# Seven block products for the second product of a pair of chunks, with the output weights held still

## The chip, the core and the metric

The kernel runs on one core of a Trainium2 chip. The metric is the device time of a run in microseconds (us). The core's engines work side by side and meet at semaphores: TensorE (PE, matrix products; PEld is its loading of the stationary operand), VectorE (DVE), ScalarE (ACT), GpSimd (POOL) and SyncE (SP), which issues nearly all DMA transfers here, in order.

## The reference

```
q_s = softmax of q over the head dimension      # 8 batches, 8 heads, 576 positions, 64
k_s = softmax of k over the positions
kv  = einsum('bhsd,bhse->bhde', k_s, v)
x   = einsum('bhsd,bhde->bhse', q_s, kv), heads side by side: 4608 x 512
h   = max(x @ w1, x @ w2, x @ w3)               # 768 wide
out = h @ w_out                                 # 4608 x 512, float32
```

All is float32. A product of float32 accuracy is made of three matmuls in a faster 32-bit format: each operand is split into a high part (a copy that rounds) and a low part (the difference), and low x high, high x low and high x high are summed.

## The kernel before

The 4608 rows are worked in nine chunks of 512: chunk c holds the first 512 positions of batch c, and the ninth the 64 left-over positions of all batches. Attention for a batch is done on VectorE, ScalarE, GpSimd and small matmuls, and it produces x, turned (features on partitions), for its chunk.

Chunks 0 to 2 (class Chunk) go the plain way: gate (L1049 to L1055) multiplies x with the three weights, hidden takes the maximum, and second_product (L1085 on) makes four tiles of 128 rows by 512 outputs, each of 6 x 3 matmuls. In these the piece of h is stationary and the split output weights wo (oh, ol) stream.

Chunks 3 to 8 go in three pairs (class Duo). There the product of the gate weights with both chunks is a 2 x 2 block product made of seven block products P1 to P7 in place of eight (Winograd's form of Strassen's scheme): convert makes the seven combinations of x (xb), mix_weights the combinations of weights, which go to DRAM (keep_s) beside copies of the plain split weights (keep_a); weights loads one 256 KB tile for each product into a ring of eight slots (ws), and products (L1276) issues six matmuls for each. There are nine units u of a weight and a pair of column blocks: unit u gives its four maxima once outcome has added and compared the seven results in PSUM (L1302 to L1324, on ScalarE and VectorE). The maxima stay in mm, 2 chunks x 6 column blocks x 512 rows. The second product of a pair was plain: hidden (L1362, L1364) splits mm into a ring of three tiles hs (the third one lies in the tile mix), and second multiplies each of eight tiles of 128 rows with wo (L1099), 18 matmuls of 512 columns a tile; a copy on ScalarE (L1118) and a store follow.

Four PSUM banks (pf) are shared by gates, block products and second products. Everything is a Step with an engine, a modelled cost, what it waits for, and the room it takes; Streams.run is a planner that sets the order of each engine's instructions by modelled times and by the table RANKS. Each engine, and SP's queue of transfers, then works strictly in that order. Up to a planned time (SPARE) the planner fills gaps of TensorE at the start with products for nothing (L509), as long as the small PSUM bank isn't in use.

Of the kernel before, what the change touches and what calls it, by code (L numbers as in the profile page):

```python
# [8 lines left out]
F32 = mybir.dt.float32  # L9
# [25 lines left out]
SPARE = 4.4, 11.5, 42.0, 0.65  # L35
# [163 lines left out]
class Streams:  # L199
# [3 lines left out]
    def __init__(self, rooms, queued):  # L203
# [7 lines left out]
        self.queues = 0.0  # L211
        self.landed = [0.0] * DMA_LANES
        self.spare = None
        self.added = 0
        self.lane = 0

    def add(self, gen, rank, inc=0.0):
# [1355 lines left out]
```

## Time and profile before

| | |
|---|---|
| three runs | 648.65, 648.71, 650.1 us (median 648.71) |
| the profiled execution | 646.05 us, its span 644.2 us |
| TensorE's mean granted clock | 0.997 |
| TensorE, VectorE, ScalarE, GpSimd busy | 98%, 66%, 48%, 9% of the span |
| DMA | 137.88 MB, mean 214 GB/s |

The profiled execution is the source of all rows below. A share of busy time is a mean over stages: up to about 50 us the core loads weights and makes the first x, then come the plain chunks (to about 287 us), and then three times the first products of a pair and its second product (363 to 403, 486 to 522 and 606 to 641 us). Matmuls are pipelined, so one of 512 columns shows some 390 ns while they follow each other at about 230 ns.

### The profile page before, as it was taken

To read this page: it belongs to the slowest core of one execution; us is meant where nothing else is said; L and a number is where in the kernel's file an instruction comes from. 1 tells how busy PE (TensorE), PEld (TensorE's weight loads), DVE (VectorE), ACT (ScalarE), POOL (GpSimd) and SP (SyncE) were. 2 spreads that over 40 slices of the span, in tenths; PEclk is the share of its full clock that TensorE was granted. 3 is DMA by queue.
4 is the path that set the end of the run, shared out by engine and by line. 5 is a ranking of instruction groups with operands and counts; after the bars stand their busy time and mean duration, and the time that the engine had idled before them with its cause. 6 is when DMAs were issued, how large, how long until landed. Compare 5 with 4: busy or idle time off the path is not lost.

```text
span 644.2 us, 9789 instructions
## 1 busy us (share of the span) xinstructions
PE 629.7 (98%) x3460; PEld 506.7 (79%) x3460; DVE 423.1 (66%) x750; ACT 309.7 (48%) x678; POOL 58.0 (9%) x57
## 2 busy tenths in 40 slices
PE   6889999999999999999999999999999999999997
PEld 5757877888777787777877877888887888888886
DVE  8988986498997988988666889342425812243420
ACT  5998374235565655855453674322223622213131
POOL 1343333110010000010010000000000000000000
PEclk9999999999999999999999999999999999999999
DMA  8976476798767568999889534576663136666122
GB/s 330 394 246 253 153 229 242 260 342 270 233 222 268 193 206 249 338 293 351 261 279 301 161 117 139 170 240 192 193 191 114 57 127 195 193 195 195 36 65 66
DMA packets 89169, 137.88 MB, mean 214 GB/s; under 512 B 7200, under 2 KB 54816, under 8 KB 86432
## 3 DMA queue, kind: packets, MB, share of 16 engines
q1 hardware_dynamic: 89040, 137.12, 64.8%
q8 instruction: 28, 0.46, 0.3%
q10 hardware_dynamic: 80, 0.13, 0.1%
q14 instruction: 21, 0.17, 0.1%
HBM read 97.12 MB, written 33.03 MB: 202 GB/s over the span
## 4 chain that ended last, share of the span: by engine, by line
PE 74%; DVE 10%; DMA 9%; ACT 3%; issue 1%; SPq 1%; DVEq 0%; ACTq 0%
PE pf L1276 37%; PE pf L1099 18%; PE pf L1052 14%; DMA wst<-in_w_dram 3%; DMA kt<-in_k_rows_dram 2%; DMA bdf<-keep_w 2%; DVE tb L870 1%; PE pa L746 1%; DVE xb L1209 1%; PE pa L969 1%; DMA qT<-tb 1%; DVE bdf L1165 1%; DMA qt<-in_q_rows_dram 1%; DVE xf L1213 1%; DVE mix L1171 1%
## 5 line engine op out<-in xcount | busy, mean ns | idle before, releaser
L1276 PE MATMUL pf<-xb,ws 128*128 128x512 f32 x1134 | 260.8, 390 | 0.2 <-DVE mm L1305 0.2
L1276 PEld LDWEIGHTS pf<-xb,ws 128*128 128x128 f32 x1134 | 212.0, 188 | 45.3 <-DVE mm L1305 0.7
L1052 PE MATMUL pf<-x,wa 128*128 128x512 f32 x648 | 158.6, 399 | 1.0 <-ACT x L949 0.8
L1052 PEld LDWEIGHTS pf<-x,wa 128*128 128x128 f32 x648 | 120.4, 189 | 30.3 <-issue 1.9
L1305 DVE TENSOR_TENSOR mm<-pf,mm 128x512 f32<-128x512 f32 x36 | 24.8, 690 | 88.7 <-PE pf L1276 88.5
L1099 PE MATMUL pf<-oh,hs 128*128 128x512 f32 x192 | 59.4, 390 | 0.0
L1324 ACT COPY pf<-pf 128x512 f32<-128x512 f32 x27 | 15.4, 572 | 84.5 <-PE pf L1276 84.5
L857 ACT ACTIVATE qt<-qt,qs 128x64 f32<-128x64 f32 x171 | 43.4, 336 | 8.7 <-DVE qs L851 6.2
L1099 PEld LDWEIGHTS pf<-oh,hs 128*128 128x128 f32 x192 | 36.0, 188 | 7.7
L570 POOL TENSOR_TENSOR wx<-wx,wst 128x512 int32<-128x512 int32 x24 | 36.0, 1526 | 62.4 <-issue 22.2
L1118 ACT COPY m<-pf 128x512 f32<-128x512 f32 x31 | 18.1, 585 | 44.4 <-PE pf L1099 30.9
L716 POOL PARTITION_ALL_REDUCE kma<-km x24 | 18.5, 773 | 215.4 <-DVE km L713 165.8
L1099 PE MATMUL pf<-ol,hs 128*128 128x512 f32 x96 | 37.7, 393 | 0.0
L870 DVE STREAM_TRANSPOSE tb<-qt 128x576 f32<-128x576 f32 x24 | 30.2, 1272 | 3.3 <-DMA qT<-tb 2.2
L1317 ACT COPY u<-pf 128x512 f32<-128x512 f32 x27 | 15.8, 586 | 32.0 <-PE pf L1276 32.0
L1099 PE MATMUL pf<-oh,mix 128*128 128x512 f32 x96 | 30.2, 395 | 0.0
L1064 DVE TENSOR_TENSOR m<-pf,m 128x512 f32<-128x512 f32 x36 | 24.6, 683 | 8.0 <-PE pf L1052 8.0
L1099 PE MATMUL pf<-ol,h_h 128*128 128x512 f32 x72 | 28.5, 395 | 0.0
L1099 PE MATMUL pf<-oh,h_l 128*128 128x512 f32 x72 | 28.1, 390 | 0.0
L1099 PE MATMUL pf<-oh,h_h 128*128 128x512 f32 x72 | 28.0, 389 | 0.0
L1364 DVE TENSOR_TENSOR hs<-mm,hs 128x512 fp32r<-128x512 f32 (+1 forms) x32 | 16.9, 552 | 13.5 <-ACT hs L1362 13.5
L1317 ACT COPY s<-pf 128x512 f32<-128x512 f32 x27 | 15.8, 587 | 19.4 <-PE pf L1276 16.8
(165 smaller groups left out, 837.5 us busy)
## 6 DMA issues: line engine op xcount, KB each, us to landing
ws<-keep_s SPq DMA_DIRECT2D x108, 256.0 KB, 3.1
ws<-keep_a SPq DMA_DIRECT2D x81, 256.0 KB, 3.1
wst<-in_w_dram SPq DMA_DIRECT2D x12, 1024.0 KB, 7.8
keep_a<-wa SPq DMA_DIRECT2D x12, 768.0 KB, 6.8
keep_s<-mix SPq DMA_DIRECT2D x9, 1024.0 KB, 6.1
vt<-in_v_rows_dram SPq DMA_DIRECT2D x24, 325.0 KB, 4.8
kt<-in_k_rows_dram SPq DMA_DIRECT2D x12, 640.0 KB, 6.4
qt<-in_q_rows_dram SPq DMA_DIRECT2D x12, 576.0 KB, 4.7
```

What stands on the lines that cost most here:

```text
L570: nc.gpsimd.tensor_add(out=x.bitcast(I32)[:, at], in0=x.bitcast(I32)[:, at], in1=low.bitcast(I32)[:, at])
L716: nc.gpsimd.partition_all_reduce(kma, km, P, bass_isa.ReduceOp.max)
L857: nc.scalar.activation(out=rows3[:, s, :], in_=rows3[:, s, :], func=AF.Copy, scale=qs[:, s : s + 1])
L870: nc.vector.transpose(out=tb[:, self.m].rearrange("p e (c s) -> p s e c", s=QS), in_=self.qt.rearrange("p s (e c) -> p s e c", e=2),)
L1052: nc.tensor.matmul(out=ps, lhsT=l[:, cc, js], rhs=r, start=(cc == 0 and t == 0), stop=(cc == NC - 1 and t == 2))
L1064: nc.vector.tensor_max(out=m, in0=self.m.pop((j, i)), in1=m)
L1099: nc.tensor.matmul(out=po, lhsT=l, rhs=r[:, j, :], start=(j == 0 and i == 0), stop=(j == NJ - 1 and i == 2))
L1118: nc.scalar.copy(out=o, in_=po)
L1276: nc.tensor.matmul(out=bank[on], lhsT=w[:, k, a], rhs=x[:, b, k], start=(i == 0 and p in ("P1", "P5")), stop=(i == 5), skip_group_check=True,)
L1305: nc.vector.tensor_max(out=m, in0=bank[on], in1=m)
L1317: nc.scalar.copy(out=f, in_=bank[on])
L1364: nc.vector.tensor_tensor(out=o[:, 1, jj], in0=mm[:, h, jj, ts], in1=o[:, 0, jj].bitcast(F32), op=ALU.subtract)
```

## The change

The second product of a pair is now a 2 x 2 block product as well: two chunks by two halves of the hidden blocks (three blocks each), and two halves of the outputs. It is made of P1 to P7 with seven combinations of mm as moving operands (operands: a subtraction where one is needed, then a split on ScalarE and VectorE, in pieces of 512 and 1024 columns), and combinations of output weights as stationary ones. Each product has two column halves v, each with nine matmuls of 512 columns into one PSUM bank, in the order of turned_order. rows adds and copies the results; they come out turned (outputs on partitions) and go to an output of their own, which is put back into rows outside the timed run.

P1 and P2 and P4 use wo as it is. The mixed output weights are made by mix_weights in three more units, from the joined output weights kept in DRAM (keep_o), and stored in keep_t; P7's take the place of parts of wo once chunk 2 is done, and P5's, P6's and P3's are loaded for each pair into two tiles so (384 KB each). The ring ws has seven slots in place of eight, and the operands lie in the tiles of x, of xb, of mix and of bdf. The gate weights are laid out and kept in whole blocks, so that a plain tile is loaded in pieces of 2 KB in place of 512 bytes. Products for nothing may go on to 120 us of planned time, then with zeros into a gate's open bank. The table RANKS is new throughout.

```diff
-SPARE = 4.4, 11.5, 42.0, 0.65
+SPARE = 4.4, 11.5, 120.0, 0.65
...
-        if n > 0 and not self.taken.get("sm"):
+        if n > 0 and (self.open or not self.taken.get("sm")):
...
-    ws = [place(f"ws{i}", [P, 2, 2, P], F32R, W_AT + 57344 + 2048 * i) for i in range(8)]
+    ws = [place(f"ws{i}", [P, 2, 2, P], F32R, W_AT + 57344 + 2048 * i) for i in range(7)]
...
+    NK = NJ // 2
...
+    so = [place(f"so{i}", [P, NK, 2, P], F32R, W_AT + 24576 + 3072 * i) for i in range(2)]
...
     keep_w = [dram.tile([P, NC, 2, P], F32, name=f"keep_w{u}") for u in range(9)]
+    keep_o = dram.tile([P, NJ, DM], F32, name="keep_o")
+    keep_t = dram.tile([P, 2, 2, 2, NK, 2, P], F32, name="keep_t")
...
+    turned_order = [
+        (p, v) for p, v in zip("P1 P1 P5 P2 P5 P2 P6 P6 P7 P7 P3 P3 P4 P4".split(), (0, 1, 0, 0, 1, 1) + (0, 1) * 4)
+    ]
...
+                st.open = [ps] if cc < NC - 1 else []
...
+        for u in range(9 + NK):
+            j = u - 9
+            after = ["left", *([("plain", u)] if j < 0 else [("plain", NU + j // 2), ("plain", NU + (j + NK) // 2)])]
+            yield Step(
+                "S", 0.55, [*after, ("low_mix", u - 1) if u else None], kb=(128, 4096) if j < 0 else (256, 2048)
+            )
...
+            yield Step("S", 0.55, kb=(128, 8192) if j < 0 else (1024, 1024), gives=("mixed", u))
...
+                nc.sync.dma_start(
+                    out=keep_t[:, :, :, :, j].rearrange("p r c v t n -> p (r c v) (t n)"),
+                    in_=mix.rearrange("p r c t n -> p (r c) (t n)"),
+                )
+        for hl in range(2):
+            yield Step(
+                "S", 0.6, [("mixed", 8 + NK), *(("y", PAIRED - 1, t, NJ - 1) for t in range(4))], gives=("mixed_in", hl),
+                kb=(768, 512),
             )
+            for v in range(2):
+                nc.sync.dma_start(
+                    out=wo[hl][:, 0:NK, (2 * v + 1) * P : (2 * v + 2) * P].bitcast(F32), in_=keep_t[:, 1, 0, v, :, hl],
+                )
...
+                yield Step("S", 0.37, after, take=[("ws", (c, p, u))], gives=("w", c, p, u), kb=(128, 2048))
+                src = keep_a[i][:, 2 * jp + r, 2 * cc : 2 * cc + 2] if kind == "a" else keep_s[u][:, r, cc]
+                nc.sync.dma_start(
+                    out=slot.rearrange("p k t n -> p (k t n)"), in_=src.rearrange("p k t n -> p (k t n)")
+                )
...
+        def operands(self):
             c = self.c
...
+            b11, b12 = (mm[:, h, 0:NK] for h in range(2))
+            b21, b22 = (mm[:, h, NK:NJ] for h in range(2))
+            parts = (slice(0, 1), slice(1, NK))
+            top = [[("m", c, 2)], [("m", c, 2), ("m", c, 5)]]
+            end = [[("m", c, 5)], [("m", c, 8)]]
+            free = {
+                0: [("Y", c - 2, "P7", 1)] if c > PAIRED else [("y", PAIRED - 1, t, NJ - 1) for t in range(4)],
+                1: [("Y", c - 2, "P3", 1)] if c > PAIRED else [("mixed", 8 + NK)],
+                2: [("gates", c)], 3: [("gates", c)], 4: [("Y", c, "P1", 1)], 5: [("Y", c, "P5", 1)],
+                6: [("Y", c, "P6", 1)],
+            }
+            def split(x, src, k, after):
+                n = CH * (1, NK - 1)[k]
+                yield Step("A", act(n), [*after, *free[x]])
+                to = self.pieces(x)
+                nc.scalar.copy(out=to[0][k], in_=src[:, parts[k]])
+                yield Step("V", dve(n), gives=("op", c, x, k), port="V")
+                nc.vector.tensor_tensor(out=to[1][k], in0=src[:, parts[k]], in1=to[0][k].bitcast(F32), op=ALU.subtract)
+            def sub(o, x, y, k, after, gives):
+                yield Step("V", dve(CH * (1, NK - 1)[k]), after, gives=(gives, c, k), port="V")
+                nc.vector.tensor_tensor(out=o[:, parts[k]], in0=x[:, parts[k]], in1=y[:, parts[k]], op=ALU.subtract)
+            gens = []
+            for k in range(2):
+                gens += [
+                    (0, split(0, b11, k, top[k])),
+                    (1, sub(b12, b12, b11, k, top[k], "t1")),
+                    (1, split(1, b12, k, [("t1", c, k)])),
+                    (2, split(2, b21, k, end[k])),
+                    (3, sub(b12, b22, b12, k, [*end[k], ("t1", c, k), ("op", c, 1, k)], "t2")),
+                    (3, split(3, b12, k, [("t2", c, k)])),
+                    (4, sub(b11, b12, b11, k, [("t2", c, k), ("op", c, 0, k)], "t3")),
+                    (4, split(4, b11, k, [("t3", c, k)])),
+                    (5, split(5, b22, k, [("t2", c, k)])),
+                    (6, sub(b21, b21, b12, k, [("t2", c, k), ("op", c, 2, k)], "t4")),
+                    (6, split(6, b21, k, [("t4", c, k)])),
+                ]
+            return gens
+        def turned_weights(self):
+            c = self.c
+            for n, p in enumerate(("P5", "P6", "P3")):
+                _, r, cc = WINO[p]
+                for v in range(2):
+                    yield Step(
+                        "S", 0.4, [("mixed", 8 + NK), ("P2", c, 8)], take=[("so", (c, p, v))], gives=("so", c, p, v),
+                        kb=(128, 3072),
+                    )
+                    nc.sync.dma_start(
+                        out=so[v].bitcast(F32).rearrange("p k t n -> p (k t n)"),
+                        in_=keep_t[:, r, cc, v].rearrange("p k t n -> p (k t n)"),
+                    )
+        def second(self):
+            c, bank = self.c, self.bank
+            OPERAND = {"P1": 0, "P5": 1, "P2": 2, "P6": 3, "P7": 4, "P3": 5, "P4": 6}
+            for p, v in turned_order:
+                on = ({"P1": "a", "P2": "a", "P5": "c", "P3": "c"}.get(p, "b"), v)
+                x = OPERAND[p]
+                need = {"P1": None, "P5": None, "P2": "s1", "P6": "seed", "P7": "u2", "P3": "s5", "P4": "c22"}[p]
+                to = [i for hl in zip(*self.pieces(x)) for i in [hl]]
+                col = 2 * v + (p in ("P4", "P7"))
+                for k in range(2):
+                    after = [("op", c, x, k)]
+                    take = ()
+                    if k == 0:
+                        after += [("Y2", c, need, v)] if need else []
+                        after += [("so", c, p, v)] if p in ("P5", "P6", "P3") else []
+                        after += [("mixed_in", hl) for hl in range(2)] if p == "P7" else []
+                        take = [("pf", (c, "y", v + 2 * (p == "P5")))] if not need else ()
+                    yield Step(
+                        "T", 3 * (1, NK - 1)[k] * f32r(CH), after, take=take, gives=("Y", c, p, v) if k else None,
+                        free=[("so", (c, p, v))] if k and p in ("P5", "P6", "P3") else (),
+                    )
+                    if take:
+                        bank[on] = pf.tile([P, CH], F32, name="pf")
+                    for kk in range(0, 1) if k == 0 else range(1, NK):
+                        at = slice(col * P, (col + 1) * P)
+                        for i, (a, b) in enumerate(((1, 0), (0, 1), (0, 0))):
+                            if p in ("P5", "P6", "P3"):
+                                w = so[v][:, kk, a]
+                            else:
+                                w = wo[a][:, kk + (NK if p in ("P2", "P4") else 0), at]
+                            nc.tensor.matmul(
+                                out=bank[on], lhsT=w, rhs=to[k][b][:, kk - k],
+                                start=(kk == 0 and i == 0 and not need), stop=(kk == NK - 1 and i == 2),
+                                skip_group_check=True,
+                            )
+        def rows(self, v):
+            c, bank = self.c, self.bank
+            s1, s5v = self.s1[v], self.s5[v]
+            last = c + 2 > B and v == 1
+            def copied(on, f, after, gives, take=()):
+                yield Step("A", act(CH), after, gives=("Y2", c, gives, v) if gives else None, take=take, rank=-1000.0)
+                if take:
+                    bank[on] = pf.tile([P, CH], F32, name="pf")
+                    nc.scalar.copy(out=bank[on], in_=f)
+                else:
+                    nc.scalar.copy(out=f, in_=bank[on])
...
+            def alone(on, h, r, after, free):
+                yield Step("A", act(CH), after, take=[("tmp", (c, "y", v, r))], free=[free], rank=-1000.0)
+                o = tmp.tile([P, CH], F32, name="m")
+                nc.scalar.copy(out=o, in_=bank[on])
+                yield from store(h, r, o, [("tmp", (c, "y", v, r))])
+            def added(on, f, r, after, gives, free=()):
+                yield Step("V", dve(CH), after, gives=("Y2", c, gives, v), free=free)
+                nc.vector.tensor_tensor(out=f, in0=bank[on], in1=f, op=ALU.add)
+                yield from store(1, r, f)
+            y = lambda i: ("pf", (c, "y", i + v))
+            return [
+                copied(("a", v), s1, [("Y", c, "P1", v), ("d12", c, 8), ("d22", c, 8)], "s1"),
+                copied(("c", v), s5v, [("Y", c, "P5", v)], "s5"),
+                alone(("a", v), 0, 0, [("Y", c, "P2", v), ("Y2", c, "s1", v)], y(0)),
+                copied(("b", v), s1, [("Y2", c, "s1", v)], "seed", take=[y(4)]),
+                copied(("b", v), s1, [("Y", c, "P6", v)], "u2"),
+                added(("b", v), s5v, 1, [("Y", c, "P7", v), ("Y2", c, "s5", v)], "c22"),
+                added(("c", v), s1, 0, [("Y", c, "P3", v), ("Y2", c, "u2", v)], "c12", [y(2)]),
+                alone(("b", v), 0, 1, [("Y", c, "P4", v)], y(4)),
+            ]
...
```

## Rows read from the trace of the kernel before

**Rows 1.** The page, part 1: busy time, share of the span, instructions, by engine.
```profile
PE 629.7 (98%) x3460; PEld 506.7 (79%) x3460; DVE 423.1 (66%) x750; ACT 309.7 (48%) x678; POOL 58.0 (9%) x57
```

**Rows 2.** The page, part 4: shares of the chain that ended last.
```profile
PE 74%; DVE 10%; DMA 9%; ACT 3%; issue 1%; SPq 1%; DVEq 0%; ACTq 0%
PE pf L1276 37%; PE pf L1099 18%; PE pf L1052 14%; DMA wst<-in_w_dram 3%; DMA kt<-in_k_rows_dram 2%; DMA bdf<-keep_w 2%; DVE tb L870 1%; PE pa L746 1%; DVE xb L1209 1%; PE pa L969 1%; DMA qT<-tb 1%; DVE bdf L1165 1%; DMA qt<-in_q_rows_dram 1%; DVE xf L1213 1%; DVE mix L1171 1%
```

**Rows 3.** The chain in order of time: start us, us, what.
```profile
93.44 8.43 DMA wst<-in_w_dram
...
264.58 2.27 DVE xb L1209 x2
...
286.58 0.64 DVE mm L1305
...
521.80 84.33 PE pf L1276 x372
...
609.53 31.05 PE pf L1099 x135
```

**Rows 4.** Waits of TensorE, 103 to 641 us: total, times, longest.
```profile
PE pf L1052 <- ACT x L949: 0.8, 1, 0.8
PE pf L1276 <- DVE mm L1305: 0.2, 1, 0.2
```

**Rows 5.** Windows of the start: length, busy by engine (instructions), granted clock, DMA.
```profile
43.00:46.80 3.80, 2.10 (x26) 1.51 (x26) 3.07 (x8) 3.74 (x8) 1.29 (x1) 1.00 0.89 277
46.80:50.50 3.70, 3.70 (x13) 2.40 (x9) 3.56 (x7) 3.26 (x7) 0.00 (x0) 0.54 0.91 310
```

**Rows 6.** Windows from 287 us, line 1099 alone: busy, weight loads, clock, DMA.
```profile
606.00:641.00 35.00, 33.37 (x144) 26.83 (x143) 1.00 0.21 53
sum 354.00, PE 101.18 PEld 80.89; mean PE 16.86 PEld 13.48
```

**Rows 7.** Windows of the stages, all instructions, columns as in rows 5.
```profile
173.00:200.00 27.00, 27.00 (x164) 21.55 (x163) 23.28 (x52) 17.21 (x48) 3.13 (x4) 1.00 0.77 255
200.00:230.00 30.00, 30.00 (x220) 23.24 (x219) 27.46 (x58) 18.83 (x51) 1.41 (x2) 1.00 0.69 230
230.00:287.00 57.00, 57.00 (x338) 45.26 (x336) 50.11 (x89) 35.66 (x80) 3.82 (x5) 1.00 0.83 266
287.00:363.00 76.00, 75.77 (x464) 60.09 (x464) 54.83 (x108) 40.13 (x105) 5.51 (x7) 1.00 0.91 284
363.00:403.00 40.00, 40.00 (x230) 31.38 (x229) 36.66 (x59) 23.75 (x50) 0.00 (x0) 1.00 0.43 132
403.00:486.00 83.00, 83.00 (x367) 68.69 (x366) 30.65 (x44) 22.14 (x40) 0.00 (x0) 1.00 0.64 198
```

**Rows 8.** Groups by line and form: operation, count, busy us, mean ns, idle before.
```profile
L1305 DVE TENSOR_TENSOR mm<-pf,mm 128x512 f32<-128x512 f32 x36 | 24.8, 690 | 88.7 <-PE pf L1276 88.5
L1209 DVE TENSOR_TENSOR xb<-xf,xb 128x1024 fp32r<-128x1024 f32 x18 | 21.6, 1220 | 3.9 <-ACT xb L1207 3.9
L1207 ACT CAST xb<-xf 128x1024 fp32r<-128x1024 f32 x18 | 18.7, 1052 | 3.2 <-DVE xf L1213 3.1
L1317 ACT COPY u<-pf 128x512 f32<-128x512 f32 x27 | 15.8, 586 | 32.0 <-PE pf L1276 32.0
L1165 DVE TENSOR_TENSOR bdf<-bdf 128x256 f32<-128x256 f32 x36 | 15.4, 427 | 4.1 <-DMA bdf<-keep_w 3.8
L1364 DVE TENSOR_TENSOR hs<-mm,hs 128x512 fp32r<-128x512 f32 (+1 forms) x32 | 16.9, 552 | 13.5 <-ACT hs L1362 13.5
```

**Rows 9.** DMA issues, 287 to 363 us, then 522 to 606 us: count, KB, landing.
```profile
ws<-keep_s SPq DMA_DIRECT2D x30, 256.0 KB, 5.7
ws<-keep_a SPq DMA_DIRECT2D x21, 256.0 KB, 6.0
...
ws<-keep_s SPq DMA_DIRECT2D x31, 256.0 KB, 3.0
ws<-keep_a SPq DMA_DIRECT2D x24, 256.0 KB, 2.9
```

More of the change, by code (lines that the diff above doesn't have):

```diff
@@ L214, in __init__ @@
         self.added = 0
+        self.open = []
         self.lane = 0
@@ L352, in linear_attention_then_maxout_ffn @@
     out: bass.AP,
+    out_turned: bass.AP,
 ):
@@ L1187, in __init__ @@
             self.order = wino_order
-            self.tiles = [(1, t) for t in range(4)] + [(0, t) for t in range(4)]
+            self.s1 = (u2, s5)
+            self.s5 = (s7, s6)
         def x(self, h):
@@ L1327, in ago, with stored @@
                 return (what, c, u - 1) if u else None
+            def stored(v):
+                return ("out", c - 2, 0, 1, v) if u == 0 and c > PAIRED else None
             def met():
@@ L1348, in all_gates @@
             yield Step("-", 0.0, [("P4", self.c, 8), ("P3", self.c, 8)], gives=("gates", self.c))
-        def hs_at(self, t):
-            return in_hs.index((self.c, t)) % 3
-        def hidden(self, t):
-            c = self.c
-            h, q = self.tiles[t]
-            ts = slice(q * P, (q + 1) * P)
-            after = [("mixed", 8)] if self.hs_at(t) == 2 else []
-            for part, jj in enumerate((slice(0, 4), slice(4, NJ))):
-                n = (jj.stop - jj.start) * P
-                yield Step("A", act(n), [("m", c, 5), ("m", c, 8) if part else None, *after], take=[("hs", (c, t))] if not part else ())
-                o = hs[self.hs_at(t)]
-                nc.scalar.copy(out=o[:, 0, jj], in_=mm[:, h, jj, ts])
-                yield Step("V", dve(n), gives=("hl", c, t, part), port="V")
-                nc.vector.tensor_tensor(
-                    out=o[:, 1, jj], in0=mm[:, h, jj, ts], in1=o[:, 0, jj].bitcast(F32), op=ALU.subtract
-                )
@@ L1368, in second, with pieces @@
-        def second(self, t):
-            h, q = self.tiles[t]
-            at = self.hs_at(t)
-            yield from second_product(
-                self.c, t, lambda j: (hs[at][:, 0, j], hs[at][:, 1, j]), lambda j: [("hl", self.c, t, 0 if j < 4 else 1)],
-                self.c + h, q, last=self.c + 2 > B and t == 7, done=("hs", (self.c, t)),
-            )
+        def pieces(self, x):
+            if x in (0, 4):
+                return [[op_a[:, t, ks] for ks in (slice(0, 1), slice(1, NK))] for t in range(2)]
+            if x in (1, 5):
+                hi = mixes[0].rearrange("p r c t n -> p (r c t n)").rearrange("p (k n) -> p k n", n=CH).bitcast(F32R)
+                return [[hi[:, 0:1], hi[:, 1:3]], [hi[:, 3:4], op_b]]
+            to = op_c if x == 2 else op_d
+            return [[to[:, t, ks] for ks in (slice(0, 1), slice(1, NK))] for t in range(2)]
@@ new lines, in rows, with store @@
+        def rows(self, v):
[7 more added lines that the diff above has]
+                    nc.scalar.copy(out=bank[on], in_=f)
+                else:
+                    nc.scalar.copy(out=f, in_=bank[on])
+            def store(h, r, o, free=()):
+                if last and (h, r) == (0, 1):
+                    yield Step("S", 0.55, kb=(128, 2048))
+                    for i, queue in enumerate((nc.sync, nc.scalar)):
+                        rows = slice(i * LEFT, (i + 1) * LEFT)
+                        queue.dma_start(out=out_turned[c - PAIRED + h, 2 * v + r, rows, :], in_=o[rows, :])
+                    return
+                yield Step("S", 0.42, kb=(128, 2048), gives=("out", c, r, h, v), free=free, rank=-1000.0)
+                nc.sync.dma_start(out=out_turned[c - PAIRED + h, 2 * v + r], in_=o)
+            def alone(on, h, r, after, free):
[18 more added lines that the diff above has]
+            ]
@@ L1500, in linear_attention_then_maxout_ffn @@
         st.add(d.all_gates(), 0.0)
-        for t in range(8):
-            st.add(d.hidden(t), -1000.0 + t)
-            st.add(d.second(t), r + 50 + t)
+        st.add(d.second(), r + 50)
+        st.add(d.turned_weights(), r - 1500.0)
+        for x, g in d.operands():
+            st.add(g, -1000.0 + x)
+        for v in range(2):
+            for g in d.rows(v):
+                st.add(g, -1500.0)
     with tc.manual_schedule():
```

163 lines of the change are left out of this document (82 added, 81 removed), and 189 rows, old and new, of the table RANKS.

## The prediction

> **What bounds the kernel now.** I read the page's busy shares first: TensorE is busy for 98% of the span, VectorE for 66% [rows 1]. A busy matmul is pipelined, so the share alone proves little; the chain that ended last is the second view, and 74% of it is TensorE, with the first products of the pairs, the second products and the plain gates as its three largest lines [rows 2]. The third view is that chain in order of time: from the first pair's products to the end it is matmul upon matmul, 372 first products in 84.33 us (0.2267 us each), then 135 second products in 31.05 us (0.2300 each) and the last stores [rows 3]. The waits of TensorE between 103 and 641 us add up to 1.0 us [rows 4]. So for the last 540 us a matmul taken out is worth its pitch, as long as nothing else becomes late. Two places are different. Before 51 us TensorE waits for weights and attention, and right after a stretch in which it was busy 2.10 of 3.80 us its granted clock reads 0.54 for 3.7 us, that is mostly the lower of the levels 1.2 and 2.4 GHz [rows 5]. And from 173 to 363 us VectorE and the DMA engines are nearly full beside a full TensorE: VectorE 23.28 of 27, 27.46 of 30, 50.11 of 57 us, DMA shares up to 0.91 [rows 7]. The chain itself runs through VectorE just ahead of 287 us [rows 3]: there two resources are tied.
>
> **What is removed.** A pair's second stage has 8 tiles of 6 x 3 matmuls, 144; three pairs, 432; a window on the last pair counts its 144 [rows 6]. Seven products, two column halves each, three blocks deep, three terms: 7 x 2 x 3 x 3 = 126 a pair, 378. So 54 matmuls of 512 columns go. The pitch of that stage is 0.2300 us in the chain (135 in 31.05) [rows 3]; I take it: **-12.4 us**. Bounds: 12.2 at the pitch of the first products (0.2267), 12.6 by the busy time of that line over all windows (101.18/432 = 0.2342) [rows 6]. The 378 that stay stream other tiles, and could run at either pitch: 378 x 0.0033 or 0.0042, 1.2 us less or 1.6 more; I take 0.
> The Trainium skill ("TensorE: Matmul & The Clock Gate", Back-to-back issue gap) gives 512/2.4 + 2.5 = 216 ns for an isolated stream; by it the term would be 11.7 us. The rows are higher in every stage here, so they decide.
>
> **What is added on VectorE and ScalarE.** Out go the splits of mm into hs: VectorE 16.9 us for 32 of 48 [rows 8], so 8.5 us a pair. In come, per pair, seven operand splits and four subtractions of three chunk-columns each (512 and 1024 wide, 0.69 and 1.22 us), 11 x 1.91 = 21.0 us, and four additions into the outputs, 2.8 us: 23.8 us, net +15.3. The first two operands and the first subtraction need only the sums of the earlier blocks, so 5.7 us lie under the first products, where VectorE has 52 of 83 us free in the second pair and 21 of 76 in the first [rows 7]. The other 18.1 us, and the next pair's conversion (7 splits and 4 subtractions of 1.22 us, 13.4), share a second stage of 126 x 0.23 = 29 us; the last two splits, 2.4, are needed only under the next products. That is 29.1 us of work by busy times in 29.0 us. Busy times overlap (in the chain two of 1024 take 2.27 us and one of 512 takes 0.64 [rows 3]), so it fits, barely. In the first pair attention is there too: the 40 us window had VectorE busy 36.66 [rows 7]. Part of that is attention for the last batch, which is needed a pair later, and under the second pair's products VectorE has 52 us idle for it. I cost it below, not at nothing.
> ScalarE makes 12 copies a pair in place of 8, and VectorE the four additions. The new chain with the shortest cover is that of P6: when P2's half ends, ScalarE copies it out, the bank comes free, ScalarE copies the seed into it, and only then P6's half starts; the other half of P6 (9 x 0.23 = 2.07 us) is all that covers it. Two copies of 0.59 [rows 8] and three hand-overs of 0.05 (287.22 to 287.27 in [rows 3]) to, as an allowance, 0.2 us make 1.3 to 1.8 us: 0 if ScalarE is free, up to 0.8 us a pair if a 1.05 us cast [rows 8] is in front. I take 0.
>
> **What is added on the DMA queues.** Three more mixings: write 1.5 MB of output weights, read them, write 3 MB mixed, 0.8 MB back in, some 6.8 MB; and 18 loads of 384 KB (7 MB) later. VectorE pays 3 x (4 x 0.43 + 2 x 0.69) = 9.3 us for the mixing [rows 8]. Only the first pair's P5 needs them (at about 365 us), and between 173 and 363 us VectorE is idle 34 us. DMA: the 287 to 363 window moves 284 GB/s at a share of 0.91, so 312 GB/s when full; 6.8 MB cost 22 us of full queues, against 32 us of free share between 173 and 363 (6.2 + 9.3 + 9.7 + 6.8) [rows 7]. It fits at a price: gate weights land in 5.7 to 6.0 us there against 2.9 to 3.0 in the quiet third pair [rows 9], and the ring for them shrinks from 8 slots to 7, so 6 x 1.36 = 8.2 us pass from a free slot to its use, not 9.5. Loads of 512-byte and of 2 KB pieces land alike in both windows [rows 9], so the whole blocks save no wait. For the first pair I take **+1.0 us** (bounds 0 and 10: all 22 us of transfers in the windows of 57 and 76 us, with 16.5 free, would be 5.5 late, and half of VectorE's 9.3 may add to it; nearer to 0, since TensorE waited 0.2 us there [rows 4]).
> The shortest cover among the new loads: the second half of P6 needs a slot that the second half of P5 frees, with 18 matmuls, 4.14 us, between. A 256 KB load lands in 2.9 to 3.0 us in the quiet pair, 5.7 to 6.0 in the busy one [rows 9]; 128 KB more at 312 GB/s add 0.4. So 3.4 fits, 6.1 is 2.0 late. I take **+0.8 us** (the first pair, whose second stage had a DMA share of 0.43 [rows 7], in between; the others in time); bounds 0 and 6. These loads stand in SP's queue among the stores of the second products, behind instructions that wait for a ScalarE copy, and the next pair's gate weights stand behind them.
> The Trainium skill ("DMA: Bandwidth & Descriptors", Anatomy of one DMA) fits about 2.0 us plus bytes at 436 GB/s on another queue path, 2.9 us for 384 KB, so no wait at all; the rows at 256 KB already read as much, so I hold to them.
>
> **The start.** Idle gaps of TensorE up to 120 us (planned time) are now filled with matmuls of zeros into an open bank. If the clock stays up, the 3.7 us at 0.54 shrink by 3.7 x 0.46 = 1.7 us. Against it: fillers in gaps that aren't there hold real work up at some 0.2 us each, and the order is new, which I can't read from rows. I take half the gain, **-0.8 us**; bounds -4 (the 1.7 us of clock, the 1.7 us of idle in the 3.80 us window, and a little of the order) and +3 (a dozen misplaced fillers). The three slices of output weights now hold their staging slots until they are stored; the next slice's own load (8.43 us in [rows 3]) covers that: 0. The end keeps its shape, a ScalarE copy and two half stores: 0.
>
> **Sum.** -12.4 + 1.0 + 0.8 - 0.8 = -11.4. The profiled execution took 646.05 us (span 644.2), so 634.65 there. It stands 2.66 us under the median of 648.71; against that the forecast is **637.3 us**.
>
> **Rivals.**
> A, the first pair waits: the added transfers and VectorE work delay conversions or weights by 5 to 10 us. For it: DMA 0.91 and the VectorE chain into 287 us. Against: TensorE waited 0.2 us there with 5.7 us landings, and attention for the last chunk can move. 637.3 + 4 to + 9: 641 to 646, 644 as its middle. Chance 0.17.
> B, the evacuation round trip becomes the bound, and the kernel is slower. Place: P6, P7 and P4 in all three pairs, 6 halves each, 18; each waits for a result of the product before it while only one half of 2.07 us covers. It decides from a round trip over 2.07 us: two copies, a 1.05 us cast in front and three hand-overs of 0.2 are 2.8, so 0.75 x 18 = 13.5 us; with a 512-wide cast more, 3.4, and 24 us: 651 to 661, 655 as its middle. For it: 16 evacuations in 29 us in place of 8 in 33. Against: the first products have the same pattern with only 1.36 us of cover, and TensorE lost 0.2 us there [rows 4]. Chance 0.10. The Trainium skill ("Trainium Kernel Development and Optimization", Best Practices) says on this side that what speeds up TensorE does not speed up PSUM evacuation.
> C, all of the additions hide and the start gains too: 637.3 - 1.8 - 1.7 to 3.2 more at the start, about 633, and 631 with the faster pitch as well. Chance 0.11.
> My forecast, with 633.5 to 641 as its own range: 0.62.
>
> **Range and chances.** 632 to 645.5 leaves out B (0.10), the top of A (0.03) and the lowest of C (0.04). A measurement of this kernel tells 0.3%, about 2 us. Faster by more: 0.62 + 0.11 + 0.14 of A = 0.87; within: 0.02 of A; slower: B and 0.01 of A, 0.11.
>
> **What will show it.** The page should count 378 matmuls in the second products of the pairs, and their three stages should last about 29 us each against some 33.5 busy now. TensorE's waits after 103 us should stay under 4 us; if P6 is late behind its stationary tiles or behind a ScalarE copy, the load or the evacuation was mis-costed. The granted clock near 47 us should read 1.00. A gap of TensorE around 275 to 300 or in the first pair behind gate weights would be A; regular gaps of about a microsecond in each second stage would be B. A pitch of those 378 away from 0.23 us would break the main term.

## The result, and the profile after

The changed kernel took 639.97 us (median of 4 runs, 637.41 to 641.25) beside 648.68 us for the kernel before (4 runs, 647.35 to 650.1): a ratio of 0.986, 95% interval 0.9824 to 0.9897, 8.7 us less. Run again unaltered beside two sets of experiments it gave 0.9904 (0.9866 to 0.9942) and 0.9907 (0.9877 to 0.9938), 7.0 and 5.6 us less. The forecast, 637.3 us, is 0.9824: the direction was right and half to three quarters of the size, and 2.7 to 5.8 us of the predicted 11.4 are missing. The profiled execution of after took 641.25 us (span 639.5), the longest of its four, that of before 646.05, less than any of its four, so the two profiles differ by 4.8 us only.

The page of after, part 1, as in [rows 1]:

```profile
PE 619.6 (97%) x3430; PEld 497.8 (78%) x3430; DVE 472.8 (74%) x797; ACT 330.6 (52%) x693; POOL 52.8 (8%) x55
```

TensorE is busy 10.1 us less, VectorE 49.7 us more. The windows on the second product's line alone (now 1491), one for each pair, answer to [rows 6] (TensorE and weight loads busy with their instructions, granted clock, DMA share, GB/s):

```profile
360.00:405.00 45.00, 30.14 (x126) 23.42 (x126) 1.00 0.82 266
480.00:523.00 43.00, 29.65 (x126) 23.50 (x126) 1.00 0.56 173
600.00:640.00 40.00, 29.22 (x126) 23.65 (x126) 0.98 0.35 112
sum 128.00, PE 89.02 PEld 70.57; mean PE 29.67 PEld 23.52
```

The 378 matmuls are there, 126 a pair, in about 29.7 us a stage. The waits of TensorE from 100 to 641 us (total, times, longest) answer to [rows 4]:

```profile
PE pf L1129 <- DVE ol L611: 2.9, 1, 2.9
PE pf L1315 <- DMA ws<-keep_s: 2.4, 3, 1.1
PE pf L1315 <- DMA ws<-keep_a: 0.8, 1, 0.8
PE pf L1315 <- DVE s L1348: 0.5, 1, 0.5
PE pf L1315 <- ACT u L1356: 0.4, 1, 0.4
```

That is 7.0 us where there were 1.0, and none of it in the second product of a pair (line 1491; line 1129 is the second product of the plain chunks). The chain in order of time (start, us, what) shows both places; it answers to [rows 3]:

```profile
94.67 11.06 DMA wst<-in_w_dram
...
109.31 1.23 DVE ol L611
...
110.59 1.67 PE pf L1129 x6
...
297.42 7.54 DMA ws<-keep_s
...
319.63 7.45 DMA ws<-keep_a
...
335.72 8.88 DMA ws<-keep_s
...
523.32 81.60 PE pf L1315 x360
...
608.32 26.87 PE pf L1491 x117
```

The last slice of output weights lands in 11.06 us in place of 8.43, and TensorE waits for its split. In the first pair's products the chain passes three times through a 256 KB load of gate weights, where before it was matmuls alone; from 350 us it is TensorE again. The windows, columns as in [rows 5, 7], say what is full there:

```profile
43.00:46.80 3.80, 3.31 (x25) 2.89 (x24) 2.69 (x8) 3.76 (x8) 0.00 (x0) 1.00 0.67 235
46.80:50.50 3.70, 3.70 (x19) 2.73 (x18) 3.63 (x7) 3.67 (x8) 0.00 (x0) 1.00 0.97 328
287.00:363.00 76.00, 71.90 (x399) 56.21 (x398) 61.24 (x115) 42.26 (x111) 2.84 (x4) 1.00 0.95 293
363.00:402.00 39.00, 39.00 (x224) 30.21 (x223) 37.12 (x52) 25.24 (x40) 2.53 (x2) 1.00 0.84 271
```

From 287 to 363 us the DMA engines are busy 0.95 of the time (0.91 before) and VectorE 61.24 of 76 us (54.83 before); TensorE loses 4.1 us there. From 363 us on TensorE loses nothing, though VectorE has 37.12 of 39 us to do. The granted clock near 47 us reads 1.00 where it read 0.54.

### The profile page after: what moved, and what is told of

It is laid out like the page before. It is cut to its first block, busy times and chain, and to the rows that moved or that the text cites. A ratio compares the mean times of both kernels' runs of the same rounds, so it can differ in the third digit from the quotient of the medians.

```text
span 639.5 us, 9836 instructions
## 1 busy us (share of the span) xinstructions
PE 619.6 (97%) x3430; PEld 497.8 (78%) x3430; DVE 472.8 (74%) x797; ACT 330.6 (52%) x693; POOL 52.8 (8%) x55
## 4 chain that ended last, share of the span: by engine, by line
PE 80%; DMA 11%; ACT 3%; DVE 2%; issue 2%; SPq 1%; ACTq 0%
PE pf L1315 35%; PE pf L1082 20%; PE pf L1491 14%; PE pf L1129 5%; DMA wst<-in_w_dram 3%; DMA bdf<-keep_w 3%; DMA ws<-keep_s 3%; PE pa L775 2%; PE pa L998 2%; DMA ws<-keep_a 1%; DMA kt<-in_k_rows_dram 1%; ACT qe L842 1%; PE pa L970 1%; PE sm L802 1%; DMA vt<-in_v_rows_dram 1%
## 5 line engine op out<-in xcount | busy, mean ns | idle before, releaser
L745 POOL PARTITION_ALL_REDUCE kma<-km x24 | 19.9, 831 | 247.9 <-DVE km L742 194.0
L597 POOL TENSOR_TENSOR wx<-wx,wst 128x512 int32<-128x512 int32 x24 | 32.1, 1361 | 72.5 <-issue 35.6
L875 ACT ACTIVATE qt<-qt 128x576 f32<-128x576 f32 x24 | 16.4, 685 | 33.7 <-DVE qt L866 32.9
L856 DVE TENSOR_REDUCE qm<-qt 128x9 f32<-128x576 f32 x24 | 17.5, 749 | 10.6 <-DMA qt<-in_q_rows_dram 10.4
L1491 PE MATMUL pf<-mix,so 128*128 128x512 f32 x84 | 25.1, 397 | 0.0
L1256 DVE TENSOR_TENSOR xb<-xf,xb 128x1024 fp32r<-128x1024 f32 x18 | 21.7, 1217 | 3.9 <-DMA out_dram<-s 2.9
L1428 DVE TENSOR_TENSOR mm<-mm 128x512 f32<-128x512 f32 (+1 forms) x24 | 22.4, 952 | 0.1
L1491 PE MATMUL pf<-op_a,oh 128*128 128x512 f32 x72 | 22.2, 389 | 0.0
```

Of the source, the lines that this page charges most:

```text
L597: nc.gpsimd.tensor_add(out=x.bitcast(I32)[:, at], in0=x.bitcast(I32)[:, at], in1=low.bitcast(I32)[:, at])
L1256: nc.vector.tensor_tensor(out=xb[i][:, 1], in0=src, in1=xb[i][:, 0].bitcast(F32), op=ALU.subtract)
L1428: nc.vector.tensor_tensor(out=o[:, parts[k]], in0=x[:, parts[k]], in1=y[:, parts[k]], op=ALU.subtract)
L1491: nc.tensor.matmul(out=bank[on], lhsT=w, rhs=to[k][b][:, kk - k], start=(kk == 0 and i == 0 and not need), stop=(kk == NK - 1 and i == 2), ...
```

## The experiments

A control, and what it is worth. `c0_after` and `c0_again` are the changed kernel unaltered, on the chips of the runs beside them.

> The changed kernel unaltered, as the control for the three runs beside it and for the four earlier experiments. If the earlier ratio of 0.986 is a property of the kernel, it takes 0.986 of the kernel before here too (0.983 to 0.989), about 636.5 us against 645.5; TensorE's waits behind the output weights and behind the streamed gate weights after 100 us add up to 4 to 7 us. If the ratio hangs on the chip or the day, it lies outside that range.

> The changed kernel unaltered once more, as the control on the chip of the three runs beside it. Its ratio to the kernel before was 0.986, and 0.9904 beside the runs without the added transfers; between 0.984 and 0.992 is expected here.

Measured: 639.74 and 639.84 us against 646.7 and 645.43 before. The first ratio, 0.9904, lies above the range expected, though its interval reaches into it; the second, 0.9907, lies inside its own. TensorE's waits after 100 us were 5.6 and 4.3 us in these two, at the same places as the 7.0 above but in other shares: what the waits cost varies from run to run. In `c0_again` gate weights are the smaller part of them:

```profile
PE pf L1129 <- DVE ol L611: 0.9, 1, 0.9
PE pf L1315 <- ACT mm L1341: 0.7, 1, 0.7
PE pf L1315 <- DVE s L1348: 0.7, 1, 0.7
PE pf L1315 <- DMA ws<-keep_a: 0.7, 1, 0.7
...
```

The kernel before differs between the sets too. In 38 of its 59 executions beside the experiments TensorE's mean granted clock was 0.999 or more, and they took 644.8, 646.0 and 644.9 us (medians on three chips); in the other 21 it was 0.992 to 0.997, and they took up to 651.59 us. The profile in [rows 5], with its 3.7 us at 0.54 and a mean of 0.997, is one of the second sort.

**54 matmuls back** (`a1_terms`): the three products on plain output weights get their low x low term, the sole change of work.

```diff
-                        for i, (a, b) in enumerate(((1, 0), (0, 1), (0, 0))):
+                        for i, (a, b) in enumerate(((1, 0), (0, 1), *(((1, 1),) if p in ("P1", "P2", "P4") else ()), (0, 0))):
...
```

> The changed kernel with a fourth term (low x low) in P1, P2 and P4 of the second stages: 18 matmuls of 512 columns more in each pair, 54 in all, as many as the change took out; the order of every other instruction is the same. Theory 1, the gain is the matmuls taken out: each costs its pitch, 54 x 0.23 = 12.4 us, so about 652.4 us, above the kernel before. Rival, the second stages are bound by operand splits or evacuations and the gain came from the new order elsewhere: the added matmuls hide in part, under 6 us, 640 to 646.

Measured: 650.4 us, 1.0069 of before (1.0045 to 1.0092). On that chip the run `a4_ring8` (below), which does the changed kernel's own work, took 637.79: 12.6 us between them, 0.233 us a matmul. Against the three ratios of the unaltered kernel (0.986 to 0.9907) it is 10.5 to 13.5 us. A matmul in this stage is worth its pitch within that spread; the main term stands.

**Fillers** (`a2_nofill`, the changed kernel with the old limits; `b1_fill`, the kernel before with the new ones).

```diff
-SPARE = 4.4, 11.5, 120.0, 0.65
+SPARE = 4.4, 11.5, 42.0, 0.65
...
-        if n > 0 and (self.open or not self.taken.get("sm")):
+        if n > 0 and not self.taken.get("sm"):
```

> The changed kernel with the products for nothing as before (up to 42 us, none into an open gate bank); nothing else in any engine's order differs. Theory 1: the granted clock falls to about 0.5 for some microseconds near 45 us, which costs 1.7 us there, but TensorE then arrives later at the output weights, for which it waits 2.9 us at 107.7 us, so the run is the same within 0.7 us (640 to 640.7). Rival, the fillers carry a part of the gain: 1.7 to 4 us slower, 641.7 to 644.

> The kernel before with one part of the change alone: products for nothing up to 120 us of planned time, then into an open bank; the planned order is otherwise identical. Theory of the clock, by my term: the stretch of 3.7 us at 0.54 near 47 us is granted 1.00, and 1.7 us go (0.9970 to 0.9985 of the kernel before, 1 to 2 us). Rival (as the run of the changed kernel without the fillers reads): they carry 4 to 5 us, 0.992 to 0.994. Second rival (the order of before has its gaps elsewhere): no gain, within 0.5 us, or a loss of up to 2 us by products for nothing in front of real work.

Measured: `a2_nofill` 641.41 us, 0.9937 (0.991 to 0.9964), 3.6 us above `a4_ring8` beside it and some 2 us above what the controls' ratios would give there, so in the rival's 1.7 to 4; it is widely spread (637.61 to 647.12, at mean clocks of 0.993 to 1.000). `b1_fill` 645.7 us, 0.9982 (0.9961 to 1.0002), 1.0 us below before, which the interval doesn't prove. The windows near 47 us, of `a2_nofill` and then of `b1_fill`:

```profile
43.00:46.80 3.80, 1.52 (x7) 1.15 (x8) 2.69 (x8) 3.76 (x8) 0.00 (x0) 0.90 0.68 239
46.80:50.50 3.70, 3.70 (x14) 2.86 (x13) 3.63 (x7) 3.36 (x6) 0.00 (x0) 0.64 1.00 410
```

```profile
43.00:46.80 3.80, 3.29 (x38) 2.48 (x36) 3.02 (x9) 3.74 (x8) 1.29 (x1) 1.00 0.84 273
46.80:50.50 3.70, 3.70 (x19) 2.67 (x18) 3.63 (x7) 3.15 (x6) 0.00 (x0) 1.00 0.91 324
```

Without fillers the busy time falls to 1.52 of 3.80 us and the granted clock behind it to 0.64, between the levels of 1.2 and 2.4 GHz; with them it reads 1.00, in the order of before too. There the first output-weight products begin at 108.88 us in place of 110.44, 1.56 us, which is the 1.7 us worked out from the clock's row; at the end of the two profiles 0.8 us of it are left (643.4 against 644.2). In time the gain is smaller still, since most executions of before have the full clock already: all twelve of `b1_fill` read 0.999 or more, and their 645.7 us is what before takes at the full clock on that chip (646.0). `a2_nofill` is 2.15 us behind `a4_ring8` at an output-weight product (110.64 against 108.49), and 1.8 of them are there at 49 us, in the stretch of the lower clock. The about 1.5 us behind that product are within its spread and were not settled.

**The output weights' lateness** (`a3_keepheld`, `d1_heldlate`): the first two 1 MB stores of kept gate weights, which share the queues with the last slice's load, are issued later; behind the last slice's store, or behind the fifth and sixth of their kind.

```diff
...
+                kept.append(store)
+                if len(kept) > 2:
+                    store()
+                if len(kept) == 6:
+                    kept[0]()
+                    kept[1]()
...
```

(The diff is that of `d1_heldlate`, with the store as a function; `a3_keepheld` holds every store until the last slice is stored.)

> The changed kernel with its first two 1 MB stores of split gate weights issued later on SP's queue, behind the store of the third output-weight slice; the rest of the order is the same. Theory 1: the last load of output weights took 11.06 us because these stores shared the queues with it; without them it lands in at most 8.5 us, TensorE's wait at 107.7 us falls from 2.9 to under 0.7 us, and the run gains 2 to 2.9 us: 637 to 638. Rival, the splitting on ScalarE, GpSimd and VectorE is what is late, or the stores collide again further on: under 0.7 us, 639.3 to 640.

> The changed kernel with the first two stores of kept gate weights issued behind the fifth and sixth of them, past the attention loads that the earlier version had blocked; all else identical. Theory of the late output weights: the third slice lands in about 7 us in place of 11, the 2.9 us wait of TensorE in front of the first output-weight products goes, nothing new stands in front of the attention loads, and the time falls by 2 to 3 us against the unaltered kernel. Rival (the stores only move): the two stores collide with the next transfers around 120 to 130 us (query loads, attention output, mixing) and TensorE waits there for 2 us or more, so that the time is within 1 us of the unaltered kernel or above it.

Measured: `a3_keepheld` 644.67 us, 0.9977 (0.9958 to 0.9995): slower than the changed kernel. Its largest wait, and its chain:

```profile
PE pa L1048 <- ACT ke L764: 6.4, 1, 6.4
```

```profile
95.27 6.97 DMA wst<-in_w_dram
...
111.87 0.78 SPq L1163
112.70 1.20 SPq L1163
113.94 1.25 SPq L1163
115.30 1.19 SPq L696
116.60 1.20 SPq L1028
117.84 9.97 DMA vt<-in_v_rows_dram
```

The load did land in 6.97 us and the wait in front of the output-weight products (2.9 us in after) was gone, as the theory had it. But the held stores (line 1163) then stood on SP's queue in front of the attention's loads and filled the DMA engines in front of them: a load of 325 KB took 9.97 us, and TensorE stood 6.4 us in front of transposes that it meets in order. Behind that stand its granted clock reads 0.50:

```profile
125.00:132.00 7.00, 0.56 (x4) 0.17 (x3) 4.05 (x8) 1.51 (x3) 0.00 (x0) 0.87 1.04 402
132.00:136.00 4.00, 4.00 (x12) 3.32 (x13) 2.63 (x6) 2.19 (x4) 1.00 (x1) 0.50 0.85 278
136.00:140.00 4.00, 4.00 (x25) 3.59 (x24) 2.06 (x3) 0.65 (x2) 0.00 (x0) 0.87 0.91 237
```

That is 2.5 us more (4 x 0.50 and 4 x 0.13, an estimate from these rows), and all twelve runs have a mean clock of 0.993 to 0.995. `d1_heldlate` avoids both: its last slice lands in 6.9 us, no wait is left at the output weights, and it took 638.54 us, 0.987 (0.984 to 0.99), against 0.9904 for the control beside it. That is 1.2 us less, which the overlapping intervals don't prove, and the two profiles end alike (636.7 and 636.8 us); the 2 to 3 us expected were not there, since the control waited 0.8 us at that place and not 2.9.

**Ring size** (`a4_ring8`): eight slots for the gate weights as before, planned as seven, so that the order is the same.

```diff
...
-    ws = [place(f"ws{i}", [P, 2, 2, P], F32R, W_AT + 57344 + 2048 * i) for i in range(7)]
+    ws = [place(f"ws{i}", [P, 2, 2, P], F32R, W_AT + 57344 + 2048 * i) for i in range(8)]
...
-    s7 = place("s7", [P, CH], F32, W_AT + 57344 + 2048 * 7)
+    s7 = place("s7", [P, CH], F32, BD_AT + 4096)
...
```

> The changed kernel with eight slots for the gate weights of the pairs in place of seven (one tile is moved to make room), planned as for seven, so that the order of every engine is the same. Theory 1, the slots: TensorE's waits for gate weights in the first pair (3.2 us) fall to under 1 us and the run gains 2 to 3 us: 637 to 638. Rival, the DMA engines are full there (share 0.95) and the loads are late whatever the slots: waits of 2.5 us or more stay, gain under 0.7 us.

Measured: 637.79 us, 0.987 (0.9841 to 0.9898), within the intervals of the changed kernel's own ratios. The time alone settles nothing: the 637 to 638 us expected came, but on a chip where the kernel before is 3.2 us faster too, and no unaltered run stood beside it. TensorE's waits tell more: 4.8 us after 100 us, 0.9 of them for gate weights, where the three profiles of the unaltered kernel have 4.3 to 7.0 and 0.7 to 3.2. No gain of the eighth slot is seen in them. The latest gate weight took 10.4 us to land there, longer than the 9.5 us that eight slots cover; a gain of a microsecond is not excluded.

**The added transfers** (`a6_notransfer`; `e1_mixpool`, half of them). In `a6_notransfer` the output weights are neither stored nor read back for mixing, and the mixed ones not stored; the loads of mixed tiles read other data. `e1_mixpool` does the whole computation: GpSimd adds the high and the low part that lie in SBUF, and only the stores of mixed weights remain.

```diff
...
-                nc.sync.dma_start(
-                    out=bdf.rearrange("p n c -> p (n c)").rearrange("p (c n) -> p c n", c=2),
-                    in_=keep_o[:, j : j + NK + 1 : NK],
+                both = [t[:, j : j + NK + 1 : NK].bitcast(F32) for t in wo]
+                nc.gpsimd.tensor_add(
+                    out=bdf.rearrange("p n c -> p (n c)").rearrange("p (c n) -> p c n", c=2), in0=both[0], in1=both[1]
                 )
...
```

> The changed kernel without the transfers of the output weights for mixing: not stored, not read back, the mixed ones not stored (the loads of mixed tiles later read other data, so the result is not the reference's); TensorE, VectorE and ScalarE do exactly the same instructions in the same order. Theory (the added 6 MB of transfers make the streamed gate weights of the first pair late, as my term of 1.0 us has it): the waits behind gate weights between 287 and 365 us go, and 1 to 4 us with them. Rival (the waits come from the new order, in which VectorE's conversions and the weights meet differently): the waits stay, and the time is within 1 us of the unaltered kernel.

> The changed kernel with the output weights not stored and not read back for their mixing: GpSimd adds the high and the low part that lie in SBUF, three additions of 1024 columns, in the place of the three reads. All other instructions and their order are the same. This takes away 1.5 of the 4.5 MB of added transfers that lie between 287 and 365 us, and the three stores of 0.5 MB around 94 to 111 us. Theory of the transfers (all of them taken away gave 6 us): a third of it in the first pair, and up to 1 us at the stores: 1.5 to 3 us faster than the unaltered kernel. Rival (GpSimd's additions, some 2.5 us each by its 1.2 to 1.5 us for 512 columns, hold VectorE up in the stretch in which it is busy 62 of 78 us): within 1 us of the unaltered kernel, or slower. Second rival (only the 3 MB of stores of mixed weights matter): within 1 us, with the waits behind gate weights as they were.

Measured: `a6_notransfer` 633.6 us, 0.9796 (0.9768 to 0.9823), 6.1 us below its control, more than the 1 to 4 expected. `e1_mixpool` 635.03 us, 0.9833 (0.9804 to 0.9862), 4.8 us below its control, with disjoint samples (633.54 to 636.24 against 638.29 to 640.23): more than the 1.5 to 3 expected, and faster than both kernels. The waits of `a6_notransfer`, then those of `e1_mixpool`:

```profile
PE pf L1305 <- ACT u L1346: 0.3, 1, 0.3
PE pf L1305 <- ACT mm L1331: 0.3, 1, 0.3
```

```profile
PE pf L1315 <- ACT u L1356: 0.6, 1, 0.6
PE pf L1315 <- DVE s L1348: 0.4, 1, 0.4
PE pf L1315 <- ACT mm L1341: 0.4, 1, 0.4
```

No wait for a DMA is left in either. Where `e1_mixpool` gains is read from the chain and TensorE's order of time, first of its control, then its own:

```profile
94.00 9.09 DMA wst<-in_w_dram
...
402.21 81.88 PE pf L1315 x360
```

```profile
106.64 0.39 PE L1129 MATMUL pf<-oh,h_l 128*128 128x512 f32 x1
107.94 0.50 PE L1129 MATMUL pf<-ol,h_h 128*128 128x512 f32 x1 [0.91 <-DVE ol L611]
```

```profile
397.86 81.82 PE pf L1315 x360
```

```profile
106.77 0.39 PE L1129 MATMUL pf<-ol,h_h 128*128 128x512 f32 x1
```

Of 4.35 us at 398 to 402 us, 1.2 are there at the seventh output-weight product (107.94 - 106.77), in front of which the control waits for the last slice; the first six begin together (105.50 and 105.41 us). The load of that slice now lands in 6.4 us in place of 9.1, without the 0.5 MB store that the control issues 0.44 us ahead of it. It takes the stores of both sizes to make it late: with the 1 MB ones away it lands in 6.9 and 6.97 us (`d1_heldlate`, `a3_keepheld`). Another 1.2 us come up to the first product of the first pair (263.68 against 266.04 us), most of them in slips of 0.2 to 0.3 us between 160 and 201 us, whose cause was not followed. The last 2.0 us are the first pair's. GpSimd's three additions took 2.46 us each, and none of the waits of TensorE above is for them.

**Both** (`e2_both`): the additions on GpSimd and the stores of `d1_heldlate`.

> The run with GpSimd's additions, and beside it the first two stores of kept gate weights issued behind the fifth and sixth. Theory: the two gains add, since one lies at 107 us and the other between 287 and 365 us: the wait in front of the first output-weight products is gone, and the time is 0.5 to 2 us below that of the run with the additions alone, 2.5 to 4 us below the unaltered kernel. Rival (the start's gain is given back in the first pair, where the same transfers then meet): no better than the additions alone.

Measured: 635.79 us, 0.9843 (0.9815 to 0.9872): no better than `e1_mixpool`. Its output-weight products begin at 105.46 us against 105.57; with the stores of 0.5 MB gone nothing was left there to gain.

**Pieces of 512 bytes** (`f1_pieces`): the 81 loads of plain tiles in pieces as before, by slots with 32 bytes behind each block.

```diff
...
-    ws = [place(f"ws{i}", [P, 2, 2, P], F32R, W_AT + 57344 + 2048 * i) for i in range(7)]
+    PIECE = P + 8
+    ws = [place(f"ws{i}", [P, 4 * PIECE], F32R, W_AT + 57344 + 16 * PIECE * i) for i in range(7)]
...
+                        out=slot.rearrange("p (i n) -> p i n", n=PIECE)[:, :, 0:P],
+                        in_=src.rearrange("p k t n -> p (k t) n"),
...
```

> The changed kernel with its 81 loads of plain gate-weight tiles in pieces of 512 bytes in place of 2 KB, by slots with a gap of 32 bytes behind each block; the same bytes, instructions and order. My prediction had it that the whole blocks save no wait: within 1 us of the unaltered kernel, and the landing of the plain tiles in the first pair within 0.5 us of that of the mixed ones (6.2 against 5.9 us). Rival (where the queues are full, smaller pieces cost queue time): the plain tiles land 1 us or more later in the first pair, TensorE waits behind gate weights 3 us or more longer, and the time is 2 to 6 us above the unaltered kernel.

Measured: 644.3 us, 0.9985 (0.9964 to 1.0006), 4.5 us above its control, which looks like the rival. The chain says otherwise:

```profile
317.06 7.77 DMA ws<-keep_a
...
340.36 10.07 DMA ws<-keep_s
...
405.79 83.34 PE pf L1321 x360
...
524.92 83.15 PE pf L1321 x360
```

The first products run at 0.2310 us a matmul (83.15/360) where the changed kernel's run at 0.2267 (81.60/360), in the quiet third pair too. 1134 of them x 0.0043 is 4.9 us, as much as the whole loss; the plain tiles land in 6.5 us beside 6.2 for the mixed ones, and TensorE waits 2.1 us for gate weights, within the 0.7 to 3.2 us of the three runs of the unaltered kernel. So the loads behave as my step on the pieces had it (0.3 us between the two kinds, and no longer waits), but as a test by time the run is poor: with the new places of the slots and blocks in SBUF the matmuls themselves became slower, and that is the loss.

## Why the prediction was right, and which terms were not

**The matmuls, -12.4: right.** 378 remain, the stage's pitch is 0.2297 us (26.87/117) against the 0.2300 taken, and putting 54 back costs 12.6 us beside `a4_ring8` (10.5 to 13.5 by the other controls). The Trainium skill ("TensorE: Matmul & The Clock Gate", Back-to-back issue gap) would have 216 ns; no stage of after shows it.

**The start, -0.8: right in size, but not for the reason given.** I took half of 1.7 us against misplaced fillers. Where the clock does fall, the whole 1.7 us come back (1.56 us in the profile of `b1_fill`), and the fillers in front of real work cost nothing that shows. But I had read the fall from one execution as if all had it: in 38 of 59 executions of before the clock stays at 0.999 or more, and there is nothing to regain. By medians the term was worth 1.0 us in `b1_fill`, not clear of its spread. This may also be why the gain was 8.7 us in the first comparison and 7.0 and 5.6 later: the kernel before took 648.68, 646.7 and 645.43 us, the changed one 639.74 to 639.97 in all three. The clocks of the first four runs of before are not on record.

**"The next slice's own load covers that: 0": wrong.** This is the step on the output-weight slices that hold their staging slots until they are stored. I asked whether the store is hidden behind the load, and it is the load that ends last. The new 0.5 MB store, the 1 MB stores and the load meet on the same queues, so the load itself takes 9.0 to 11.1 us in place of 6.4, and the chain goes through it. Price: 1.2 us in `c0_again`; TensorE's wait there was 0.8, 0.9 and 2.9 us in the three profiles of the unaltered kernel.

**The first pair, +1.0: too small.** The mechanism was named and its place was right (rival A's, 287 to 363 us), the size was not. The transfers fitted into the free share on average, as I had it, at a DMA share of 0.95 to 0.97. But each gate weight comes in step with its product, and 8.2 us pass from a free slot to its use: the latest of some 45 took 8.9, 9.2 and 9.2 us to land in the three profiles of the unaltered kernel, and 7.6 and 7.2 in `e1_mixpool` and `a6_notransfer`, where TensorE waits for none. In the kernel before it was 8.4, with 9.5 us to spend. The medians don't tell: 6.0 and 6.3 us in after as against 5.7 and 6.0 [rows 9], but 5.5 and 5.3 in `c0_again`. A mean that fits says nothing of the latest load. Nor are gate weights all: in `c0_again` 2.7 of TensorE's 3.4 us in the first pair's products are waits for results of ScalarE and VectorE, and VectorE stood 3.8 us for rows of q there, 2.0 in `e1_mixpool`. That attention's late loads are behind those waits fits, but is not shown. Price: 2.0 us by the half that `e1_mixpool` takes away; for all transfers and both places `a6_notransfer` gives 6.1 us where these two steps had 1.0, and in its profile 4.9 us of the distance to `c0_after` arise in the first pair. Which part of it is bytes and which the longer mixing chain behind a 7.4 us read, the runs don't separate.

**The tiles so, +0.8: wrong, nearly 0.** 18 loads of 384 KB landed in 3.6 us (median, 3.0 to 7.4), and the profile of after has no wait of TensorE behind them; 0.2 to 1.1 us in five other runs. The load with the shortest cover, that of P6's second half in the first pair, landed in 3.7 us, where 4.14 were to spend and I had feared 6.1. The Trainium skill ("DMA: Bandwidth & Descriptors", Anatomy of one DMA) would by its fit for another queue path, an estimate, have 2.9 us and no wait, which is nearer than my term.

**Rival B: refuted.** 16 evacuations in 29 us, and in no run a wait of TensorE behind ScalarE or VectorE in the second product of a pair: the evacuations came in time. VectorE, 37.12 of 39 us busy there in the first pair, did not bind either. **Rival C** was right that the fillers cost nothing, and wrong on the transfers.

With measured sizes the sum reads -12.6 - 1.0 + 6.1 = -7.5 us, against 5.6 to 8.7 measured. That the total came near is owed to the main term; what the transfers of `a6_notransfer` cost was put at a sixth of its size. In part it is also luck: 639.97 us lies in the forecast's own 633.5 to 641, but by the ratios of the two controls (0.9904 and 0.9907 of 648.68) it would be 642.5, inside the 641 to 646 of rival A, and it is A's mechanism that was seen. Of the signs named ahead, the 378 matmuls, stages near 29 us and the clock of 1.00 came; the bound of 4 us on TensorE's waits was broken by 0.3 to 3 us, in part in the way given there for A: gaps from about 278 us on and in the first pair, behind gate weights among others. The wait at the output weights was in none of the signs.

## What to carry to other kernels

Where the tensor engine is the chain, count instructions times pitch first; the pitch read from the chain before (0.2300 us) held after (0.2297). Then treat each added transfer as a delay of the loads already on the path at that moment, not as a share of free bandwidth: take the latest landing of the busiest window against the ring's cover, and look which load ends the chain at each place where a store is added. If data lie in SBUF in another form, an idle engine that rebuilds them (here 7.4 us of GpSimd) can be cheaper than a store and a read.

## What the runs showed of the hardware that was not expected

A stream of 512-column matmuls can run slower at a granted clock of 1.00 and without a wait. With slots 2176 bytes apart and plain blocks 544 bytes apart (`f1_pieces`) it ran at 0.2310 us, with slots 2048 and blocks 512 bytes apart at 0.2267. The kernel before loads its plain tiles in pieces of 512 bytes and also runs at 0.2267 (84.33/372 in [rows 3]), so the pieces are not the reason. Nor is the place of the tile in use: the starts of the single matmuls show 0.231 us also for P5, whose mixed tile lies, from the second unit on, at the address and with the blocks of 512 bytes that it has in the changed kernel. And the products of P3, always in the same slot, follow each other at 226 and 227 ns in every second unit and at 224 to 236 ns in the others. What in the new layout does it was not tried.

A queue that issues in order can cost more than the transfers on it: the stores held back in `a3_keepheld` took away a wait of 0.8 to 2.9 us at one place and cost 6.4 at the next, and about 2.5 more at a granted clock of 0.50 to 0.87 behind it.
